# Batch 0's attention masks from TensorE to VectorE in a planned attention and feed-forward kernel, with new planner numbers

## The chip, the core and the metric

The kernel runs on one core of one Trainium2 chip. Its engines are TensorE (PE in the profile; PEld is its weight load), VectorE (DVE), ScalarE (ACT), GpSimd (POOL) and SyncE (SP), whose queue issues all DMA transfers. The metric is the device time of one execution in microseconds, as the median of several runs; lower is better.

## The reference

```
scores = scale * q @ k.T            # 8 batches, 8 heads, 576 positions, 64 wide
masks: heads 0-3 see the last 32 positions, heads 4-7 every 4th of the last 128
attn = softmax(where(mask, scores, -1e9)) @ v
x = attn as 4608 tokens x 512
h = x @ w_in                        # 512 -> 2048
g = (a0 + a1 h + a2 h^2 + a3 h^3) / (1 + |b0||h| + |b1| h^2 + 1e-6)
out = g @ w_out                     # 2048 -> 512
```

## The kernel before

**Attention** is cut into 8 batches of 6 units; unit n of the trace's names is 6 times the batch plus its place (`u`). A unit loads `qk` and `v`, and then runs these steps, each a planned operation: scores (`qk`, PE, into two PSUM banks named `pair`, `pair_A` or `pair_B`), mask, row maximum `mx` (DVE), subtraction into `p` (DVE), exponential (ACT), row sum `sm` and its reciprocal (DVE), normalisation of `p` (POOL), transposition to `pT`, and the product with `v` (PE). The result is split into a high part `xh` (ACT) and the rest `xl`, the two float32r operands of the feed-forward products; columns that belong to the last block of tokens are kept aside as `l` and stored to DRAM as `left`.

The mask is added in one of two ways, chosen by `on_pe`. With it, PE multiplies an identity `ident_b` with the bf16 mask `mask_t` into the bank before the scores are accumulated on top (two matmuls of 128x192 a unit). Without it, `mask()` adds the mask on DVE after the scores, in one instruction or two, by the list `MASK_AT`: two pieces in units 0, 4 and 5, one in units 1, 2 and 3.

The exponential has three kinds, in the table `KIND`. Kind 0: DVE subtracts the maximum into `p`, ACT takes one exponential of `p`, DVE sums. Kind 1: ACT takes six exponentials of 64 columns straight from the bank, each with a bias and an accumulated sum. Kind 2 (all of batch 1): PE subtracts the maximum in the bank with two matmuls.

**Feed-forward** is cut into 144 tiles: a block `c` of 512 tokens by a slice `ft` of 128 hidden columns. The order starts with block 0's first 8 slices, then block 1's 16, then block 0's other 8, then blocks 2 to 8. Tile i makes the hidden product `h` (12 matmuls of 128x512, called h0, h1 and so on below), then a chain: `a` = |h|, `r` (linear, ACT), `t` (linear, ACT), `a<-r,a` (DVE or POOL), two further products on DVE (`t<-t,h`, `h<-t,na_t,h`), logarithm and exponential of `r` (ACT), and three products on DVE, the last of which (`a<-a,h`, here "the last product of the tile") gives g and frees the bank of `h`. Then `gh` = g rounded (ACT, or POOL) and `gl` = g - gh (DVE or POOL for the first 36 tiles, POOL after), and the output products `out` (12 matmuls). The weights come as raw words (`wi_raw`, `wo_raw`) and are put together by ACT, POOL and DVE (`wi_f`), then split into `wi` high and low. Weight slots of the last slices first hold batch 0's `qk` and `v`.

**The order** of all instructions on all engines is made when the program is built, by `Plan.run`: a list scheduler that takes the operation of lowest rank among those that can start first, by durations written in each `op(...)`, hop times between engines and a model of the DMA pipe; where an operation may run on more than one engine it also picks the engine. Ranks come from `due()`, which goes back from due times (`DUE`, one pair a batch), lags in tiles (`LATE`) and margins (`SLACK`). `masked` is the load of the masks, `lc` that of the six coefficients, and `coefs` makes `na_t` (DVE) and `ab_t` (ACT) from them. `pin` keeps that order on each engine, so every engine and the SP queue works strictly in it.

Of the kernel before, what the change touches and what calls it, by code (L numbers as in the profile page):

```python
# [78 lines left out]
class Plan:  # L79
# [6 lines left out]
    DMA_START, DMA_NS, DMA_RATE = 3300.0, 1750.0, 375.0  # L86
# [97 lines left out]
def tile_attention_moe(  # L184
# [29 lines left out]
    def act(o, i, func, **kw):  # L214
        pin(nc.scalar.activation(o, i, func, **kw))  # L215
# [41 lines left out]
    class Unit:  # L257
        def __init__(self, b, u):
            self.b, self.u, self.n = b, u, b * NU + u
            self.start, self.on_pe, self.by_pe = b == 0, b < ON_PE, b < BY_PE  # L260
# [248 lines left out]
        def plan(self, by, tags):  # L509
# [10 lines left out]
            if prev:  # L520
                sc = op({"PE": 1320 + 300 * self.on_pe}, 0, lambda e: (prev.av(), self.scores()), *prev.placed, prev.lv, lq, *masks)
                clear = prev.finish(sc)
            else:
                sc = op({"PE": 1130 + 320 * self.on_pe}, 0, lambda e: self.scores(), lq, *masks)
# [54 lines left out]
            if start:  # L579
                av = op({"PE": 1500}, 0, lambda e: self.av(), *self.placed, lv)  # L580
# [5 lines left out]
        def finish(self, av):  # L586
# [331 lines left out]
    for key in keys:  # L918
        plan_weights(key)
# [127 lines left out]
```

## Time and profile before

| | |
|---|---|
| median of 3 runs | 916.32 us (913.51 to 917.98) |
| the profiled execution | 916.49 us, its span 914.7 us |
| mean granted TensorE clock | 0.994 |
| PE busy | 883.2 us, 97% of the span |
| DVE busy | 742.3 us, 81% |
| ACT busy | 675.4 us, 74% |
| POOL busy | 467.7 us, 51% |
| DMA | 103.46 MB, mean 113 GB/s |

The span runs from the first to the last instruction; times in the trace count from its start. A busy share is a mean over stages with different limits, so what a change is worth is read from the stage that it changes. PE works with pipelined matmuls whose ends are modelled: a busy PE is not always a PE at its peak, and the distance between two starts tells more than the busy time.

### The profile page before, as it was taken

The page shows a single profiled execution, that of the slowest core. Times are in us where ns is not written, and L with a number is a line of the kernel's source. Part 1 is how long each engine was busy: PE and PEld are TensorE (multiplying, and loading weights), DVE is VectorE, ACT ScalarE, POOL GpSimd, SP SyncE. Part 2 cuts the span into 40 slices and gives each one's busy share as a digit, 9 for nine tenths or more (in the row PEclk, how much of TensorE's full clock was granted, in tenths as well). Part 3 has the DMA queues.
Part 4 walks back from the last instruction along what each step waited for, and adds up shares of the span by engine and source line. Part 5 has one row for each costly group of instructions (what it writes and reads, how often), then busy time and mean ns, then how long its engine had stood idle before and what let it go on. Part 6 is the DMA issues. An engine that isn't in the chain of part 4 may idle for free.

```text
span 914.7 us, 21129 instructions
## 1 busy us (share of the span) xinstructions
PE 883.2 (97%) x8153; PEld 716.1 (78%) x8153; DVE 742.3 (81%) x1312; ACT 675.4 (74%) x1092; POOL 467.7 (51%) x408
## 2 busy tenths in 40 slices
PE   5877999999999999999999999999999999999998
PEld 3755787887877878888888888888888788888876
DVE  4789999999988988788978888887779677566656
ACT  2676888877666777877787778677777688778764
POOL 2454554656635554555455555546455545444442
PEclk9989999999999999999999999999999999999999
DMA  9667460235633343334334324423333220001001
GB/s 359 240 221 249 154 234 1 99 124 190 198 99 110 110 134 118 119 111 125 115 113 127 121 83 146 129 82 85 115 95 91 61 69 1 1 1 47 0 1 47
DMA packets 85477, 103.46 MB, mean 113 GB/s; under 512 B 37376, under 2 KB 62848, under 8 KB 85376
## 3 DMA queue, kind: packets, MB, share of 16 engines
q1 hardware_dynamic: 85376, 102.11, 34.5%
q8 instruction: 64, 1.05, 0.5%
q14 instruction: 37, 0.30, 0.1%
HBM read 75.21 MB, written 26.87 MB: 112 GB/s over the span
## 4 chain that ended last, share of the span: by engine, by line
PE 75%; DVE 11%; DMA 5%; ACT 5%; issue 3%; POOL 1%; SPq 1%; DVEq 0%; POOLq 0%; ACTq 0%
PE out L212 34%; PE h L212 34%; PE pair L212 5%; DVE h L221 3%; DVE a L221 2%; DMA wi_raw<-in_w_in_dram 2%; ACT r L215 2%; DVE t L218 1%; DVE a L218 1%; DVE gl L218 1%; DMA wo_raw<-in_w_out_dram 1%; SPq L209 1%; DMA qk<-in_qk_dram 1%; ACT a L215 1%; PE pair_B L212 1%
## 5 line engine op out<-in xcount | busy, mean ns | idle before, releaser
L212 PE MATMUL h<-xh,wi 128*128 128x512 f32 x1136 | 378.1, 394 | 6.8 <-DVE a L221 6.5
L212 PE MATMUL out<-gh,wo 128*128 128x512 f32 x1136 | 353.8, 393 | 0.7 <-DVE os L218 0.7
L224 POOL TENSOR_TENSOR a<-r,a 128x512 f32<-128x512 f32 x121 | 156.6, 1294 | 241.1 <-ACT r L215 233.4
L212 PEld LDWEIGHTS h<-xh,wi 128*128 128x128 f32 x1136 | 214.5, 189 | 58.3 <-DVE a L221 12.6
L212 PEld LDWEIGHTS out<-gh,wo 128*128 128x128 f32 x1136 | 211.2, 188 | 45.9 <-DVE os L218 1.1
L212 PE MATMUL out<-gl,wo 128*128 128x512 f32 x568 | 221.8, 391 | 1.6 <-DVE gl L218 1.0
L212 PE MATMUL h<-xl,wi 128*128 128x512 f32 x568 | 222.4, 391 | 0.0
L224 POOL TENSOR_TENSOR gl<-a,gh 128x512 fp32r<-128x512 f32 x129 | 175.1, 1357 | 64.7 <-ACT gh L215 64.0
L221 DVE SCALAR_TENSOR_TENSOR h<-h,na_t,r 128x512 f32<-128x512 f32 x142 | 106.9, 753 | 111.0 <-ACT r L215 109.2
L215 ACT ACTIVATE r<-a,ln_bias 128x512 f32<-128x512 f32 x141 | 101.9, 723 | 82.8 <-POOL a L224 80.3
L215 ACT ACTIVATE r<-a,ab_t 128x512 f32<-128x512 f32 x141 | 114.7, 814 | 16.3 <-DVE a L221 14.5
L212 PEld LDWEIGHTS out<-gl,wo 128*128 128x128 f32 x568 | 106.6, 188 | 25.6 <-POOL gl L224 1.5
L212 PEld LDWEIGHTS h<-xl,wi 128*128 128x128 f32 x568 | 107.3, 189 | 21.5
L215 ACT ACTIVATE a<-h 128x512 f32<-128x512 f32 x140 | 83.5, 596 | 53.7 <-PE h L212 35.0
L215 ACT ACTIVATE t<-h,na_t 128x512 f32<-128x512 f32 x142 | 109.6, 772 | 5.0 <-PE h L212 4.6
L221 DVE SCALAR_TENSOR_TENSOR h<-t,na_t,h 128x512 f32<-128x512 f32 x142 | 107.3, 756 | 4.9
L215 ACT ACTIVATE r<-r,exp_bias 128x512 f32<-128x512 f32 x144 | 104.3, 724 | 4.7
L218 DVE TENSOR_TENSOR t<-t,h 128x512 f32<-128x512 f32 x142 | 96.6, 681 | 7.2 <-ACT t L215 7.1
L221 DVE SCALAR_TENSOR_TENSOR a<-a,r 128x512 f32<-128x512 f32 x141 | 100.2, 711 | 0.0
L221 DVE SCALAR_TENSOR_TENSOR a<-a,h 128x512 f32<-128x512 f32 x140 | 96.2, 687 | 4.8
L215 ACT ACTIVATE gh<-a 128x512 fp32r<-128x512 f32 x130 | 81.5, 627 | 23.2 <-PE out L212 14.9
L224 POOL TENSOR_TENSOR p<-p,sm 128x384 f32<-128x384 f32 x48 | 47.7, 993 | 34.3 <-DVE sm L352 28.1
(115 smaller groups left out, 712.4 us busy)
## 6 DMA issues: line engine op xcount, KB each, us to landing
qk<-in_qk_dram SPq DMA_DIRECT2D x48, 448.0 KB, 5.0
v<-in_vp_dram SPq DMA_DIRECT2D x48, 384.0 KB, 3.7
out_dram<-os SPq DMA_DIRECT2D x36, 256.0 KB, 2.3
wi_raw<-in_w_in_dram SPq DMA_DIRECT2D x16, 512.0 KB, 6.1
wo_raw<-in_w_out_dram SPq DMA_DIRECT2D x16, 512.0 KB, 6.9
results<-y SPq DMA_DIRECT2D x42, 192.0 KB, 2.4
z<-results SPq DMA_DIRECT2D x168, 48.0 KB, 2.5
turned<-u SPq DMA_DIRECT2D x36, 192.0 KB, 2.0
```

The lines of the kernel that those rows point to most:

```text
L209: pin(nc.sync.dma_start(dst, src))
L212: pin(nc.tensor.matmul(o, lhs, rhs, start=start, stop=stop, skip_group_check=free))
L215: pin(nc.scalar.activation(o, i, func, **kw))
L218: pin(nc.vector.tensor_tensor(o, x, y, op))
L221: pin(nc.vector.scalar_tensor_tensor(o, x, s, y, op0, op1))
L224: pin(nc.gpsimd.tensor_tensor(o, x, y, op))
```

## The change

Four things change.

1. `on_pe` holds for batch 1 alone; DVE adds the masks of batch 0.
2. `KIND[4]` goes from 1 to 0: unit 4's maximum is subtracted on DVE, its exponential is one ACT instruction, its sum one DVE instruction.
3. The masks' load follows the first load of all (`qk` of unit 0), and the coefficients' load and the next two loads follow the masks.
4. Durations in the plan, the DMA model, `DUE`, `LATE` and `SLACK` get other numbers. These set the order only; no instruction's work depends on them.

```
-KIND = [0, 0, 0, 0, 1, 0] + [2] * 6
+KIND = [0, 0, 0, 0, 0, 0] + [2] * 6
...
-DUE = [(-41.16, 11.47), (-146.25, 19.43), (423.68, 72.57), (61.95, 5.87), ...
+DUE = [(-44.94, 13.4), (-40.09, 42.02), (421.32, 53.66), (48.0, 2.07), ...
...
-    DMA_START, DMA_NS, DMA_RATE = 3300.0, 1750.0, 375.0
+    DMA_START, DMA_NS, DMA_RATE = 1000.0, 1700.0, 380.0
...
-            self.start, self.on_pe, self.by_pe = b == 0, b < ON_PE, b < BY_PE
+            self.start, self.on_pe, self.by_pe = b == 0, b == 1, b < BY_PE
...
-            no = op({"POOL": 790}, 0, lambda e: self.norm(e), rc)
+            no = op({"POOL": 880}, 0, lambda e: self.norm(e), rc)
...
-            low = {"DVE": sum(120 + 2 * c[1] / 0.96 for c, _ in main)}
+            low = {"DVE": sum(200 + 2 * c[1] / 0.9 for c, _ in main)}
...
-    lc = op({"SP": 60}, -39.5, lambda e: load(coef_t, coef), dma=3000)
-    masked.follows.append(lc)
+    lc = op({"SP": 430}, -39.3, lambda e: load(coef_t, coef), dma=3000)
...
+    masked.follows.append(first_loads[0])
+    for o in (lc, *first_loads[1:3]):
+        o.follows.append(masked)
```

The number behind a name's letters is the unit, the slice or the tile; the one behind the underscore is a buffer's serial number.

The start of SP's queue, before:

```order
L209 DMA qk0_110<-in_qk_dram 128x896
L209 DMA v0_112<-in_vp_dram 128x768
L209 DMA qk1_114<-in_qk_dram 128x896
L209 DMA coef_t_95<-in_coef_dram 128x6
L209 DMA mask_t_89<-in_mask_dram 128x384
L209 DMA v1_121<-in_vp_dram 128x768
```

and after:

```order
L209 DMA qk0_110<-in_qk_dram 128x896
L209 DMA mask_t_89<-in_mask_dram 128x384
L209 DMA v0_113<-in_vp_dram 128x768
L209 DMA qk1_115<-in_qk_dram 128x896
L209 DMA v1_120<-in_vp_dram 128x768
L209 DMA coef_t_95<-in_coef_dram 128x6
```

The masks move ahead of unit 0's v, and the coefficients behind unit 1's v.

SP's queue some 20 rows on, where the raw weights of slice 4 (`wi_raw4`) are loaded and unit 2's left part is stored, before:

```order
L209 DMA qk7_147<-in_qk_dram 128x896
L209 DMA wi_raw4_508<-in_w_in_dram 128x512
L209 DMA v5_510<-in_vp_dram 128x768
L209 DMA v6_512<-in_vp_dram 128x768
L209 DMA v7_514<-in_vp_dram 128x768
L209 DMA left_80<-l2_518 128x2x64
```

and after:

```order
L209 DMA qk7_206<-in_qk_dram 128x896
L209 DMA v6_210<-in_vp_dram 128x768
L209 DMA v7_238<-in_vp_dram 128x768
L209 DMA left_80<-l2_478 128x2x64
L209 DMA wi_raw4_484<-in_w_in_dram 128x512
L209 DMA left_80<-l3_522 128x2x16
```

The weight load moves from ahead of three loads to behind a store that waits for unit 2's result.

DVE in tiles 13 and 14 (the products of the chain; `wo_f8` joins the words of a weight), before:

```order
L218 TENSOR_TENSOR a13_2026<-r13_2031,a13_2026 128x512
L218 TENSOR_TENSOR gl12_2045<-a12_1972,gh12_2037 128x512
L218 TENSOR_TENSOR t13_2043<-t13_2043,h13_1994 128x512
L221 SCALAR_TENSOR_TENSOR h13_1994<-t13_2043,na_t_96,h13_1994 128x512
L221 SCALAR_TENSOR_TENSOR h13_1994<-h13_1994,na_t_96,r13_2031 128x512
L221 SCALAR_TENSOR_TENSOR a13_2026<-a13_2026,r13_2031 128x512
L221 SCALAR_TENSOR_TENSOR a13_2026<-a13_2026,h13_1994 128x512
L221 SCALAR_TENSOR_TENSOR wo_f8_2017<-wo_f8_2017,wo_raw8_1856 128x512
L218 TENSOR_TENSOR a14_2074<-r14_2080,a14_2074 128x512
L218 TENSOR_TENSOR gl13_2096<-a13_2026,gh13_2088 128x512
```

and after:

```order
L218 TENSOR_TENSOR a13_2043<-r13_2055,a13_2043 128x512
L221 SCALAR_TENSOR_TENSOR h13_2009<-t13_2048,na_t_96,h13_2009 128x512
L413 STREAM_TRANSPOSE y12_2080<-pair_85 128x2x96 x2
L381 STREAM_TRANSPOSE u14_2086<-p14_1973 128x192 x2
L221 SCALAR_TENSOR_TENSOR h13_2009<-h13_2009,na_t_96,r13_2055 128x512
L221 SCALAR_TENSOR_TENSOR a13_2043<-a13_2043,r13_2055 128x512
L221 SCALAR_TENSOR_TENSOR a13_2043<-a13_2043,h13_2009 128x512
L221 SCALAR_TENSOR_TENSOR wo_f8_2007<-wo_f8_2007,wo_raw8_1803 128x512
L218 TENSOR_TENSOR a14_2096<-r14_2102,a14_2096 128x512
L227 CAST wo8_2123<-wo_f8_2007 128x512
```

The two subtractions `gl` have left DVE (they stand in POOL's row), two attention transpositions and a weight's rounding stand between the products instead.

More of the change, by code (lines that the diff above doesn't have):

```diff
@@ L520, in plan @@
             if prev:
[L521 removed]
+                sc = op({"PE": 1320 + 700 * self.on_pe}, 0, lambda e: (prev.av(), self.scores()), *prev.placed, prev.lv, lq, *masks)
                 clear = prev.finish(sc)
             else:
[L524 removed]
+                sc = op({"PE": 1500 + 450 * self.on_pe}, 0, lambda e: self.scores(), lq, *masks)
             if self.on_pe:
@@ L531, in plan @@
                 mx = op({"DVE": 470}, 0, lambda e: self.max(True), ma)
-                sb = op({"PE": 760}, 0, lambda e: self.sub_pe(), mx, identity)
+                sb = op({"PE": 950}, 0, lambda e: self.sub_pe(), mx, identity)
                 su = ex = op({"ACT": 480}, 0, lambda e: self.exp_s(), sb)
-                sm = op({"DVE": 470}, 0, lambda e: self.sum(), ex)
+                sm = op({"DVE": 510}, 0, lambda e: self.sum(), ex)
             elif kind:
@@ L540, in plan @@
                 su = op({"DVE": 500}, 0, lambda e: self.sub(), mx)
-                ex = op({"ACT": 425}, 0, lambda e: self.exp(), su)
-                sm = op({"DVE": 470}, 0, lambda e: self.sum(), ex)
+                ex = op({"ACT": 470}, 0, lambda e: self.exp(), su)
+                sm = op({"DVE": 510}, 0, lambda e: self.sum(), ex)
             rc = op({"DVE": 300}, 0, lambda e: self.recip(), sm)
-            no = op({"POOL": 790}, 0, lambda e: self.norm(e), rc)
+            no = op({"POOL": 880}, 0, lambda e: self.norm(e), rc)
             if self.by_pe:
-                tr = op({"PE": 690}, 0, lambda e: self.transposes(), no, identity)
+                tr = op({"PE": 900 if start else 600}, 0, lambda e: self.transposes(), no, identity)
                 pl = op(BOTH, 0, lambda e: self.place(e), tr)
@@ L579, in plan @@
             if start:
[L580 removed]
+                av = op({"PE": 2000}, 0, lambda e: self.av(), *self.placed, lv)
                 av.slack = 0.0
@@ L601, in finish @@
                 if LESS[u]:
-                    ms = op({"PE": sum(60 + 2 * c[1] / 1.6 for c, _ in main)}, 0, lambda e: self.less_hi(), eh, identity)
+                    ms = op({"PE": sum(150 + 2 * c[1] / 1.4 for c, _ in main)}, 0, lambda e: self.less_hi(), eh, identity)
                     ms.slack = 0.0
@@ L611, in finish @@
             else:
-                low["POOL"] = sum(100 + 2 * c[1] / 0.49 for c, _ in main)
+                low["POOL"] = sum(130 + 2 * c[1] / 0.45 for c, _ in main)
                 el = op(low, 0, lambda e: self.evac_lo(e), eh, lock=True)
@@ L695, in plan_weights @@
             sc = op({"ACT": 600}, 0, lambda e: w_scale(key), f)
-            lw = op({"ACT": 690, "POOL": 690}, 0, lambda e: w_low(key, e), f, consts)
-            jn = op({"DVE": 680}, 0, lambda e: w_join(key), sc, lw, lock=True)
+            lw = op({"ACT": 690, "POOL": 740}, 0, lambda e: w_low(key, e), f, consts)
+            jn = op({"DVE": 710}, 0, lambda e: w_join(key), sc, lw, lock=True)
             steps = [sc, lw, jn]
@@ L700, in plan_weights @@
             steps = [op({"DVE": 335}, 0, lambda e: w_copy(key), f)]
-        hi = op({"ACT": 550, "DVE": 460, "POOL": 620}, 0, lambda e: w_hi(key, e), steps[-1], lock=True)
-        lo = op({"DVE": 602, "POOL": 1280}, 0, lambda e: w_lo(key, e), hi, lock=True)
+        hi = op({"ACT": 550, "DVE": 460, "POOL": 680}, 0, lambda e: w_hi(key, e), steps[-1], lock=True)
+        lo = op({"DVE": 625, "POOL": 1350}, 0, lambda e: w_lo(key, e), hi, lock=True)
         plan.takes(steps[0], "stage", STAGE, [lo])
```

12 lines of the change are left out of this document (6 added, 6 removed).

## Prediction

> **What bounds the kernel now.** I read the page's busy shares first, then a table of stages, then who TensorE waits for, then the rows of one stage.
>
> ```profile
> PE 883.2 (97%) x8153; PEld 716.1 (78%) x8153; DVE 742.3 (81%) x1312; ACT 675.4 (74%) x1092; POOL 467.7 (51%) x408
> ```
>
> TensorE (PE) is busy for 883.2 of 914.7 us; 31.5 us are left to win. The stages say where (columns: stretch, length, then busy us of each engine).
>
> ```profile
> 7.10:40.00 32.90, 27.10 (x722) 21.61 (x721) 23.55 (x57) 16.42 (x49) 12.30 (x14) 1.00 0.78 292
> 40.00:60.00 20.00, 15.90 (x337) 12.18 (x336) 16.64 (x38) 14.81 (x28) 8.42 (x9) 0.83 0.88 303
> 60.00:90.00 30.00, 23.29 (x284) 17.97 (x284) 27.77 (x51) 19.87 (x35) 12.68 (x15) 1.00 0.68 233
> 90.00:110.00 20.00, 19.10 (x166) 14.81 (x164) 18.60 (x32) 17.12 (x29) 12.47 (x11) 0.91 0.40 128
> 110.00:134.00 24.00, 23.68 (x194) 19.45 (x195) 23.64 (x36) 20.73 (x34) 13.10 (x11) 1.00 0.65 228
> 134.00:163.00 29.00, 28.73 (x122) 22.21 (x122) 28.05 (x43) 24.70 (x40) 13.31 (x11) 1.00 0.07 30
> 210.00:260.00 50.00, 49.47 (x578) 39.99 (x577) 45.27 (x88) 37.48 (x63) 27.19 (x28) 1.00 0.59 184
> 260.00:350.00 90.00, 89.01 (x840) 71.76 (x838) 76.19 (x139) 65.50 (x104) 48.35 (x45) 1.00 0.36 110
> ```
>
> PE's gaps before 110 us are 7.1 + 5.8 + 4.1 + 6.7 + 0.9 = 24.6 of the 31.5. Three regimes. Until 40 us everybody waits in turn: VectorE (DVE) is idle for 9.35 us of 32.9. From 60 to 134 us DVE is the bound: 27.77 of 30.0, then 18.60 of 20, then 23.64 of 24, while PE loses 6.7 us in 60 to 90. From 134 to 163 us both look full; later DVE has slack. The waits of PE name DVE too; the last row, from the timeline, is the start of h5, tile 5's hidden product:
>
> ```profile
> PE pair_A L212 <- DMA mask_t<-in_mask_dram: 7.3, 1, 7.3
> PE h L212 <- DVE a L221: 6.5, 5, 3.4
> ...
> 89.19 0.50 PE L212 MATMUL h<-xh,wi 128*128 128x512 f32 x1 [3.35 <-DVE a L221]
> ```
>
> The stage of 134 to 163 us hides a loss that no idle column shows.
>
> ```profile
> 139.16 0.50 PE L212 MATMUL h<-xh,wi 128*128 128x512 f32 x1
> 144.96 0.50 PE L212 MATMUL h<-xh,wi 128*128 128x512 f32 x1
> 150.76 0.50 PE L212 MATMUL h<-xh,wi 128*128 128x512 f32 x1
> ...
> 842.36 2.72 PE h L212 x12
> 845.08 2.72 PE out L212 x12
> ...
> 139.62 0.69 DVE L218 TENSOR_TENSOR a<-r,a 128x512 f32<-128x512 f32 x1
> 140.22 1.10 DVE L218 TENSOR_TENSOR gl<-a,gh 128x512 fp32r<-128x512 f32 x1
> 145.42 0.69 DVE L218 TENSOR_TENSOR a<-r,a 128x512 f32<-128x512 f32 x1
> ```
>
> The hidden products h13, h14, h15 start 5.80 us apart, though a tile needs 2.72 + 2.72 = 5.44 us of PE, as late in the run. DVE's own loop repeats in 145.42 - 139.62 = 5.80 us: DVE sets the pace, and 1.10 us of it is the subtraction that makes gl. So the time is PE's work plus what DVE withholds up to about 160 us.
>
> The profiled execution took 916.49 us around its 914.7 us span; the median of the runs is 916.32, 0.17 less. I sum against 916.49.
>
> **The change, part by part.**
>
> (1) The start. The masks' transfer moves from fifth to second, and the first scores no longer wait for it.
>
> ```profile
> 7.31 0.48 PE L212 MATMUL pair_A<-mask_t,ident_b 128*128 128x192 bf16 x2 [7.31 <-DMA mask_t<-in_mask_dram]
> ...
> 0.72 0.38 SPq L209 DMA_DIRECT2D qk<-in_qk_dram  x1
> DMA to landing us min/median/max: 3.2/3.2/3.2
> ...
> 3.04 0.43 SPq L209 DMA_DIRECT2D v<-in_vp_dram  x1
> DMA to landing us min/median/max: 5.2/5.2/5.2
> ...
> 9.91 0.52 ACT L215 ACTIVATE p<-p 128x384 f32<-128x384 f32 x1 [2.58 <-DVE p L218]
> ```
>
> The first qk lands at 0.72 + 3.2 = 3.9 us, so scores may begin 3.4 us before 7.31. But the coefficients now stand behind unit 1's v, which landed at 3.04 + 5.2 = 8.2 us, and ScalarE (ACT) still makes ab_t from them ahead of the first exponential, as DVE makes na_t ahead of the first sum. That exponential thus starts near 8.4 instead of 9.91: 1.5 us. Bounds: 0 (the later qk transfers pace the units anyway) and 3.4. What is late next is unit 1's qk. I take 1.5, as a head start for DVE only.
>
> (2) Masks and unit 4. PE loses twelve matmuls; DVE gains the additions, the subtraction and the sum.
>
> ```profile
> 8.62 0.50 PE L212 MATMUL pair<-mask_t,ident_b 128*128 128x192 bf16 x2
> 9.05 0.97 PE L212 MATMUL pair<-qk 64*32 64x64 f32 x48
> ...
> L218 DVE TENSOR_TENSOR pair<-pair,mask_t 128x192 f32<-128x192 f32 x2 | 0.7, 362 | 0.0
> L218 DVE TENSOR_TENSOR pair<-pair,mask_t 128x384 f32<-128x384 f32 x1 | 0.5, 541 | 0.0
> L218 DVE TENSOR_TENSOR p<-pair_A,mx 128x384 f32<-128x384 f32 x2 | 1.1, 553 | 0.0
> L348 DVE TENSOR_REDUCE sm<-p 128x6 f32<-128x384 f32 x13 | 7.1, 544 | 1.8 <-ACT p L215 1.7
> ```
>
> PE: 6 units by 9.05 - 8.62 = 0.43 us make 2.6 us, worth nothing here, since PE waits in this stage. DVE: three units with two pieces, 6 by 0.362, and three with one, 3 by 0.541, are 3.8 us; unit 4 adds 0.553 + 0.544 = 1.1 (a small scalar step that it loses is left in); together 4.9 us. ACT drops six small exponentials and their accumulator reads for one step; ACT is no bound here, so zero, covered by its 16.5 idle us before 40. Where do DVE's 4.9 us go? They must fit into 9.35 us of idle time plus the head start. Bounds: -1.5 (all fit, head start kept) and +3.4 (none fits, 4.9 - 1.5). The idle time is waiting between steps of one unit, and the masks belong to other units, so they fill it; yet each mask also lengthens its own unit's chain. I take 0.
>
> (3) The order of the ramp. Rows of both orders times the mean of their form's row say how much DVE must do before a landmark: up to the last product of tile 3 (on which h5 waits; 3.4 us is the longest wait above) 8.3 us more than before; up to tile 9 1.9 us more, with the 4.9 us of (2) inside. So apart from the masks DVE does less by tile 9, and batch 1's last unit and unit 13 are served earlier. h5 will come late by some us and tiles 6 to 10 get that back. Bounds at tile 9: +1.9 less the 1.5 of (1), so +0.4, if DVE's idle time stays as it is; 0.4 - 4.9 = -4.5 if the masks' time disappears in it. I take 0 at tile 10: the nearest rows, 90 to 134 us, show an engine with no idle time to fill.
>
> (4) Tiles 10 to 24. gl leaves DVE altogether: 12 before, none after; GpSimd (POOL) makes all 141 plain ones.
>
> ```profile
> L218 DVE TENSOR_TENSOR gl<-a,gh x9: 686/1101/1119, 116.9 to 253.5; 128x512 fp32r<-128x512 f32 x9
> L221 DVE SCALAR_TENSOR_TENSOR a<-a,r x25: 649/682/1341, 113.8 to 258.1; 128x512 f32<-128x512 f32 x25
> ...
> L224 POOL TENSOR_TENSOR gl<-a,gh 128x512 fp32r<-128x512 f32 x129 | 175.1, 1357 | 64.7 <-ACT gh L215 64.0
> ```
>
> Without gl the loop of 5.80 is 4.70, below PE's 5.44: PE sets the pace. h13 to h17 gain 5 by 0.36 = 1.8 us; bounds 0 and, if tiles 21 to 24 gain alike, 3.2. I take 2.2. POOL has room (13.31 of 29 us busy), but a gl of 1.36 us instead of 1.10 makes the path from gh to out longer; the second tile of buffers covers that.
>
> (5) After 210 us. PE idles 0.53 of 50 and 0.99 of 90 us; DVE does less, attention units start at other places. Bounds +1.5 (new collisions of the same size) and -1.5 (all gone); I take -1.1. Tiles after 100 keep their order of work in all but single rows, and so does the end: 0.
>
> Sum: 0 + 0 + 0 - 2.2 - 1.1 = -3.3, so 913.2 by the profiled execution and 913.0 against the median.
>
> **The rivals.**
>
> *The ramp shrinks (908).* If the planner's new order also closes DVE's gaps, term (3) takes its -4.5 or so: 916.5 - 3.3 - 4.5 = 908.7, with some of (1) kept 908. For it: 9.35 idle us before 40 and 3.4 more in 40 to 60. Against: these are chains of small steps over three engines, and DVE's row before h5 has grown by 8.3 us.
>
> *The slower side: weights held behind a store (921).* On SP's queue wi4 now stands behind the store of unit 2's left part, which waits for ACT.
>
> ```profile
> 15.94 0.33 SPq L209 DMA_DIRECT2D wi_raw<-in_w_in_dram  x1
> DMA to landing us min/median/max: 9.9/9.9/9.9
> 27.40 3.42 SPq L209 DMA_DIRECT2D left<-l  x2
> ...
> 36.37 0.47 SPq L209 DMA_DIRECT2D wi_raw<-in_w_in_dram  x1
> DMA to landing us min/median/max: 4.4/4.4/4.4
> ```
>
> Before it was issued at 15.94 and landed at 25.8; the store went out at 27.40. A lone transfer took 4.4 us. Behind a store as late as that one it would land at 27.8 + 4.4 = 32.2; unit 2 stands some 2 us further ahead in the new order, so I say 30.2, 4.4 us late. ACT takes its conversion in order, ahead of unit 4's evacuation and unit 5's exponential; wi6 can repeat it. If that time is not refilled before h5, the ramp ends 4.4 us later and the masks lose their cover for as long: 916.5 + 4.4 + 3.4 - 3.3 = 921. It decides if it holds ACT for over 4 us. Against: units 6 to 8 had slack on PE, and other steps are ready on DVE.
>
> *gl on POOL frees nothing (917).* The rows above show a<-a,r at 649 at least and 1341 at most: such an operation, both inputs in SBUF, can stand for up to 0.66 us beside POOL's work. If each gl of POOL blocks DVE for its whole 1.36 us instead of the 1.10 saved, the loop is 6.06 instead of 5.80, tiles 13 to 17 lose 1.3 us, and (4) turns from -2.2 to +1.3: 916.5 + 1.3 - 1.1 = 916.7, say 917. The median of 682 beside a maximum of 1341 says that few are blocked. [...]
>
> *The change does not act.* That DVE adds masks is sure; that nothing moves in the end is the middle of the other cases.
>
> **How the numbers follow.** Forecast 0.45, its own range 910.5 to 916. Ramp shrinks 0.28. gl frees nothing 0.13. Weights held 0.12. The rest, 0.02, is anything else. About 0.5%, 4.6 us, is what a measurement tells from no change: faster is below 911.7, slower above 920.9. Faster: nearly all of the second case (0.27) and a quarter of the first (0.11), 0.38. Slower: most of the weights case and a little of others, 0.12. Same: 0.50. The range 905.5 to 920 leaves out the far ends of the ramp case and the worse half of the weights case.
>
> **What the profile after would show.** (1) First scores near 4 us, first exponential near 8.4 with ACT waiting for coef_t; wrong if it still starts near 9.9. (2) DVE idle before 40 us lower by about 4; wrong if h0 and S8 move by more than 5. (3) h5 at 92 to 96 (89.2 before) and tile 13 (139.16 before) starting within 2 us of that. (4) No gl on DVE, h13 to h17 spaced by 5.44, a<-a,r still about 0.68 in the median; wrong if the spacing stays at 5.8. (5) PE idle after 210 us below 1.5. The prediction fails most likely in (3): a hand count cannot place the waits of three engines to a few us.

## The result, and the profile after

The changed kernel takes 929.81 us (median of four runs, 925.72 to 931.77), the kernel before 917.15 (913.51 to 918.58, the three runs shown and one more): a ratio of 1.0151, 95% interval 1.0130 to 1.0171. It is slower by 1.5%. The forecast was 913.0 with a range up to 920.0; the time lies outside it, on the other side of the kernel before.

The profiled execution of the changed kernel took 928.49 us, its span 926.7: 12.0 us more than before. First the page's busy shares.

```profile
PE 886.0 (96%) x8141; PEld 717.4 (77%) x8141; DVE 744.3 (80%) x1313; ACT 674.6 (73%) x1079; POOL 476.0 (51%) x419
```

PE has twelve matmuls less and is busy 2.8 us longer. DVE does 2.0 us more. Neither sum says where 12 us went, so the same stages as before follow (stretch, length, busy us of PE, its weight load, DVE, ACT, POOL, then PE's granted clock, the DMA share and GB/s).

```profile
7.10:40.00 32.90, 24.07 (x610) 18.82 (x611) 25.17 (x63) 15.84 (x37) 11.24 (x12) 1.00 0.83 300
40.00:60.00 20.00, 15.53 (x383) 11.92 (x383) 17.32 (x34) 16.09 (x33) 9.01 (x9) 0.91 0.77 269
60.00:90.00 30.00, 25.27 (x373) 19.22 (x372) 26.56 (x49) 19.82 (x36) 11.94 (x12) 0.89 0.82 278
90.00:110.00 20.00, 14.81 (x54) 11.71 (x53) 15.92 (x26) 15.16 (x26) 8.40 (x7) 0.83 0.27 83
110.00:134.00 24.00, 21.86 (x96) 17.38 (x95) 21.48 (x36) 17.95 (x29) 14.97 (x12) 1.00 0.39 125
134.00:163.00 29.00, 28.98 (x219) 23.58 (x218) 27.80 (x46) 26.27 (x44) 19.84 (x16) 1.00 0.43 149
210.00:260.00 50.00, 47.79 (x568) 37.80 (x567) 45.76 (x90) 33.22 (x55) 26.86 (x25) 1.00 0.57 177
260.00:350.00 90.00, 87.97 (x924) 71.12 (x925) 78.74 (x151) 64.50 (x104) 51.74 (x50) 1.00 0.44 131
```

From 60 to 134 us, where DVE was the full engine before (27.77, 18.60 and 23.64 us), it now has pauses: 26.56, 15.92 and 21.48. PE loses with it: 14.81 of 20 us instead of 19.10 in 90 to 110. From 134 to 163 PE is full, as the prediction wanted. After 210 us PE idles 2.2 of 50 and 2.0 of 90 us instead of 0.5 and 1.0. PE's table of waits has the largest ones (us in all, how many, the longest):

```profile
PE h L212 <- DVE a L221: 8.2, 5, 5.2
PE pair_A L212 <- DMA qk<-in_qk_dram: 5.3, 2, 4.0
PE pair L212 <- ACT r L215: 3.3, 1, 3.3
```

PE's timeline shows where they stand, and what follows a long one (start, duration, the wait ahead of it in brackets).

```profile
3.95 0.97 PE L212 MATMUL pair_A<-qk 64*32 64x64 f32 x48 [3.95 <-DMA qk<-in_qk_dram]
...
80.75 0.91 PE L212 MATMUL pair<-v,pT 64*32 64x64 f32 x45 [3.35 <-ACT r L215]
...
97.82 0.80 PE L212 MATMUL h<-xh,wi 128*128 128x512 f32 x1 [5.19 <-DVE a L221]
98.42 0.63 PE L212 MATMUL h<-xl,wi 128*128 128x512 f32 x1
...
102.69 0.63 PE L212 MATMUL h<-xh,wi 128*128 128x512 f32 x1
103.11 0.75 PE L212 MATMUL out<-gh,wo 128*128 128x512 f32 x2
...
148.33 0.39 PE L212 MATMUL h<-xh,wi 128*128 128x512 f32 x1
...
153.77 0.49 PE L212 MATMUL h<-xh,wi 128*128 128x512 f32 x1
...
220.48 0.67 PE L212 MATMUL pair<-v,pT 64*32 64x64 f32 x44 [1.65 <-DVE y L413]
```

h5 starts at 97.82 instead of 89.19, after the longest wait of the run. Its twelve matmuls then take 103.11 - 97.82 = 5.29 us; at full pace, as at 842 us in before, they take 2.72 (before, h5 took 4.40 after a wait of 3.35). So this wait costs PE twice, once idle and once slow. In all PE idles 36.8 us between its matmuls instead of 27.9, 8.9 of the 12.0 us; 2.8 are PE working longer, though 2.6 us of mask products are gone, and 0.3 stand behind its last matmul. In the rows from 40 to 110 us the granted clock withholds 0.09 x 20 + 0.11 x 30 + 0.17 x 20 = 8.5 us, in those of before 0.17 x 20 + 0.09 x 20 = 5.2; by this estimate up to 3.3 us of the longer work are the lower clock.

By landmarks the 12.0 us come as +3.8 until h0, +4.8 from h0 to h5, +0.5 to h13, -2.5 to h24, +3.8 to h40, +1.6 to the end. So 8.6 stand at h5, and all of it is still there at h13 (+9.1).

What h5 waits for is seen on DVE's timeline.

```profile
93.79 0.68 DVE L221 SCALAR_TENSOR_TENSOR a<-a,r 128x512 f32<-128x512 f32 x1
96.16 1.02 DVE L218 TENSOR_TENSOR xl<-z,xh 128x64 fp32r<-128x64 f32 x2 [1.69 <-ACT xh L215]
97.09 0.68 DVE L221 SCALAR_TENSOR_TENSOR a<-a,h 128x512 f32<-128x512 f32 x1
```

The last row is the last product of tile 3, which frees h5's bank. Its inputs were ready at 94.47, but the rest `xl` of unit 11 stands ahead of it in the list, and that waits for ACT, which waits for the transfer z of unit 11 (landed at 95.63). DVE idles 1.69 us and works 1.02 more before it turns to the row that PE needs. The PE wait at 80.75 is alike: a subtraction for unit 12 stood behind `xl` of unit 8 on DVE, which idled 1.93 us at 74.54 for that unit's z. (The table names ACT for this wait; that it is the subtraction is seen when this row is moved, below.)

On SP's queue (issues only) three weight loads have come forward into this stretch.

```profile
61.44 0.42 SPq L209 DMA_DIRECT2D wi_raw<-in_w_in_dram  x1
...
62.94 0.58 SPq L209 DMA_DIRECT2D wi_raw<-in_w_in_dram  x1
...
75.10 0.33 SPq L209 DMA_DIRECT2D wi_raw<-in_w_in_dram  x1
75.53 0.84 SPq L209 DMA_DIRECT2D z<-results  x2
```

They are `wi_raw8` to `wi_raw10`, first needed at about 165 us; before, they were issued together at 78.68 behind `wo_raw7`. DVE joins the words of two of them, and splits one, ahead of tile 3's last product. The DMA share of 60 to 90 us has gone from 0.68 to 0.82.

### The profile page after: what moved, and what is told of

The parts are those of the page before. It is cut to its first block, busy times and chain, and to the rows that moved or that the text cites. A ratio compares the mean times of both kernels' runs of the same rounds, so it can differ in the third digit from the quotient of the medians.

```text
span 926.7 us, 21150 instructions
## 1 busy us (share of the span) xinstructions
PE 886.0 (96%) x8141; PEld 717.4 (77%) x8141; DVE 744.3 (80%) x1313; ACT 674.6 (73%) x1079; POOL 476.0 (51%) x419
## 4 chain that ended last, share of the span: by engine, by line
PE 72%; DVE 10%; DMA 8%; ACT 4%; SPq 3%; issue 2%; POOL 1%; DVEq 0%; ACTq 0%; POOLq 0%
PE h L212 34%; PE out L212 33%; PE pair L212 4%; DMA z<-results 3%; SPq L209 3%; DVE h L221 2%; DMA results<-y 2%; DVE a L221 2%; ACT r L215 1%; DVE t L218 1%; DMA wi_raw<-in_w_in_dram 1%; DMA turned<-u 1%; DVE a L218 1%; DMA coef_t<-in_coef_dram 1%; DVE wo L227 1%
## 5 line engine op out<-in xcount | busy, mean ns | idle before, releaser
L224 POOL TENSOR_TENSOR a<-r,a 128x512 f32<-128x512 f32 x117 | 151.5, 1295 | 247.6 <-ACT r L215 226.9
L224 POOL TENSOR_TENSOR gl<-a,gh 128x512 fp32r<-128x512 f32 x141 | 190.7, 1353 | 60.0 <-ACT gh L215 53.1
L221 DVE SCALAR_TENSOR_TENSOR a<-a,h 128x512 f32<-128x512 f32 x140 | 96.1, 686 | 4.7
L224 POOL TENSOR_TENSOR p<-p,sm 128x384 f32<-128x384 f32 x48 | 46.2, 966 | 29.7 <-DVE sm L352 28.6
```

The costliest lines, as they stand in the source:

```text
L221: pin(nc.vector.scalar_tensor_tensor(o, x, s, y, op0, op1))
L224: pin(nc.gpsimd.tensor_tensor(o, x, y, op))
```

## The experiments

Three questions: is it the mechanism (masks and unit 4 on DVE, masks second on the queue) or the order that came with the new numbers; if the order, is it single rows, the early weights, or the weights behind the store of `left` (the prediction's own rival); and what is gl on POOL worth by itself. For all kernels but three the plan decides as usual; either some steps then emit other instructions in their old places, or the list is edited by the few moves shown before the instructions are emitted. So those differ from their parent by nothing but these rows (helpers shift the line numbers). The ratios are against the kernel before on the same chip; landmarks are the start of the hidden product of that tile in the profiled execution.

| kernel | h0 | h5 | h10 | h13 | h24 | h40 | span | ratio (95%) |
|---|---|---|---|---|---|---|---|---|
| before | 41.9 | 89.2 | 122.6 | 139.2 | 203.5 | 301.1 | 914.7 | 1 |
| after | 45.7 | 97.8 | 130.6 | 148.3 | 210.1 | 311.5 | 926.7 | 1.0151 (1.0130-1.0171) |
| *in the order of before* | | | | | | | | |
| masks_old_order | 40.8 | 87.1 | 120.9 | 137.6 | 201.9 | 299.4 | 912.3 | 0.9997 (0.9986-1.0008) |
| masks_second_old_order | 39.9 | 88.0 | 121.4 | 137.9 | 201.9 | 299.9 | 914.0 | 0.9992 (0.9977-1.0006) |
| masks_old_order_second | 42.3 | 90.2 | 123.6 | 140.1 | 204.4 | 301.7 | 914.6 | 0.9998 (0.9987-1.0009) |
| gl_pool_old_order | 41.0 | 89.3 | 125.0 | 141.5 | 204.6 | 302.4 | 916.1 | 1.0006 (0.9992-1.0021) |
| early_weights_old_order | 41.4 | 94.3 | 127.3 | 143.8 | 209.1 | 306.7 | 919.9 | 1.0068 (1.0049-1.0088) |
| *planned anew* | | | | | | | | |
| old_code_new_numbers | 48.7 | 101.2 | 137.2 | 152.7 | 224.6 | 323.9 | 936.4 | 1.0237 (1.0219-1.0256) |
| new_code_old_numbers | 41.8 | 89.8 | 122.5 | 146.4 | 210.1 | 317.3 | 931.1 | 1.0178 (1.0163-1.0194) |
| one_duration_changed | 42.1 | 91.1 | 122.2 | 140.5 | 204.0 | 308.8 | 921.9 | 1.0084 (1.0062-1.0107) |
| *in the order of after* | | | | | | | | |
| pe_masks_new_order | 47.2 | 99.4 | 130.0 | 147.6 | 209.6 | 312.8 | 925.6 | 1.0144 (1.0124-1.0165) |
| sub12_ahead_of_z8 | 45.0 | 95.6 | 126.9 | 144.7 | 206.4 | 307.7 | 921.4 | 1.0128 (1.0094-1.0162) |
| last3_ahead_of_z11 | 45.9 | 95.9 | 127.7 | 145.5 | 207.2 | 307.9 | 921.6 | 1.0099 (1.0082-1.0115) |
| both_rows_moved | 45.9 | 96.1 | 128.8 | 146.6 | 208.3 | 308.4 | 923.1 | 1.0112 (1.0092-1.0132) |
| weights_ahead_of_left | 44.9 | 97.0 | 132.2 | 149.9 | 211.7 | 313.4 | 927.4 | 1.0140 (1.0127-1.0154) |
| late_rows_moved | 44.8 | 97.7 | 132.8 | 150.4 | 212.2 | 315.7 | 931.0 | 1.0142 (1.0125-1.0160) |
| early_weights_later | 47.1 | 98.5 | 135.9 | 153.7 | 215.4 | 320.7 | 934.4 | 1.0198 (1.0176-1.0219) |
| early_weights_later_rows | 46.6 | 94.0 | 131.0 | 148.8 | 210.5 | 315.0 | 929.3 | 1.0155 (1.0132-1.0177) |
| weights_behind_z11 | 46.2 | 92.7 | 130.4 | 152.7 | 215.5 | 316.3 | 930.5 | 1.0205 (1.0186-1.0224) |
| weights_and_unit5 | 48.2 | 92.9 | 131.4 | 153.6 | 216.7 | 320.1 | 935.7 | 1.0213 (1.0190-1.0236) |

A landmark comes from one execution, and it varies: late_rows_moved has the order of after on every queue until 210 us, and its h10 still comes 2.2 us later. So differences of a landmark under some 2 us say little; the ratios carry the verdicts.

### The mechanism or the order

**masks_old_order**: the kernel before, whose order stays row for row; within it DVE adds batch 0's masks and unit 4 is kind 0.

```
-            on_pe = self.on_pe
+            on_pe = self.b == 1
...
+            if self.start:
+                self.mask()
...
-                mx = op({"DVE": 660}, 0, lambda e: self.max_bank(), ma)
+                mx = op({"DVE": 660}, 0, lambda e: (self.max(), self.sub()), ma)
```

> The planned order of before, row for row, but VectorE adds batch 0's masks ahead of each maximum and unit 4 goes by subtraction, one exponential and a sum (the mechanism alone; the mask matmuls are left out of TensorE's rows). Theory A (the loss is in the re-made order: VectorE gets 9.6 us more work ahead of h5, of which the masks and unit 4 are 4.9): VectorE is idle 16.8 us before h0, so the masks fit mostly there: h0 within 2 us of 41.9, h5 within 2.5 of 89.2, time 915 to 920. Theory B (the masks themselves cost the loss, because each lengthens its unit's chain by 0.4 to 0.7 us and VectorE is the bound later): h0 4 us later, h5 6 to 9 us later, time 922 to 929.

**pe_masks_new_order**: the reverse, the order of after with the masks on PE and unit 4 as before (`bank` is true for unit 4).

```
-            on_pe = self.on_pe
+            on_pe = self.b < ON_PE
...
-                su = op({"DVE": 500}, 0, lambda e: self.sub(), mx)
-                ex = op({"ACT": 470}, 0, lambda e: self.exp(), su)
+                su = op({"DVE": 500}, 0, lambda e: None if bank else self.sub(), mx)
+                ex = op({"ACT": 470}, 0, lambda e: self.exp_bank() if bank else self.exp(), su)
```

> The planned order of after, row for row, but TensorE adds batch 0's masks again and unit 4 takes its six small exponentials (the mechanism undone, the order kept). Theory A: little comes back, h5 stays at 96 to 98, time 926 to 930. Theory B: most comes back, h5 at 89 to 92, time 917 to 922.

915.70 against 915.45 for the first, 928.43 for the second. The mechanism costs nothing in the old order, and undoing it gives nothing measurable back in the new one (1.0144 and 1.0151 overlap). The whole loss belongs to the order. How the masks are taken up shows in the first kernel's stage:

```profile
7.10:40.00 32.90, 24.14 (x712) 20.01 (x712) 28.78 (x71) 15.22 (x39) 12.49 (x15) 1.00 0.82 309
```

DVE works 28.78 us of 32.9 instead of 23.55: 5.2 us more, all in its idle time. The second kernel's stage and its h5:

```profile
7.10:40.00 32.90, 24.11 (x613) 18.71 (x614) 20.13 (x53) 16.23 (x46) 10.99 (x12) 1.00 0.80 292
```

```profile
99.43 0.79 PE L212 MATMUL h<-xh,wi 128*128 128x512 f32 x1 [5.85 <-DVE a L221]
```

Here DVE has 5 us less to do than after has in this stage, and h5 comes no earlier (99.43 against 97.82). How much DVE has to do before h5 does not alone set when h5 starts.

**old_code_new_numbers** (code of before, numbers of after) and **new_code_old_numbers** (code of after's parts 1 and 2, numbers and load order of before) are both planned anew, as is **one_duration_changed**, the kernel before with one planned duration, that of the row sum, 10 ns longer (it stands in two places, of which one is shown).

```
-                sm = op({"DVE": 470}, 0, lambda e: self.sum(), ex)
+                sm = op({"DVE": 480}, 0, lambda e: self.sum(), ex)
```

> The kernel before with the durations, transfer model, due times, lags and margins of after, so the planner makes the order anew with TensorE's masks. Theory A: the numbers carry the loss, 922 to 932, with h5 later than 93 and waits on z loads ahead of VectorE. Theory B: about 917, h5 at 88 to 91.

> VectorE adds batch 0's masks and unit 4 is changed, planned anew with all of before's numbers and before's order of the first loads. Theory A: near before, 914 to 920. Theory B: like after, 922 to 930.

> The kernel before with one planned duration changed from 470 to 480 ns (the row sum on VectorE), so that the planner makes the order anew: the same instructions, about 300 of 1218 rows of VectorE's order in another place. Theory T (the old numbers were fitted to the old program, and any new draw of the order loses): ratio 1.005 to 1.025. Rival N (the numbers of the change are bad in themselves): 0.998 to 1.004.

937.46, 931.75 and 924.09: 2.4, 1.8 and 0.8% slower. So neither set of numbers is good or bad by itself. The old numbers fit the old program only, and even there 10 ns in one duration, which by the plan moves some 300 of DVE's 1218 rows, cost 0.84%. Each of the four orders planned anew in this study, after's own included, was slower than before's. They do not lose in the same place: new_code_old_numbers is level with before until h10 (122.5), 7.2 us late at h13 and 16.1 at h40.

**masks_second_old_order** and **masks_old_order_second** put the masks' transfer second, in before's order and in that of masks_old_order.

```
+    def edit(self):
+        self.move("masked", ahead_of=("lv", 0))
```

> The order of before, row for row, but the masks' transfer is the second on the queue. Step (1) of the prediction: the first scores start near 4.3 instead of 7.31, the first exponential near 7.3; the later qk transfers land as before, so units 2 to 5 and h0 move by less than 0.5 us and the time by less than 1 us. Rival: the head start lasts and h0 is 1.5 to 3 us earlier, and so is the end.

> The order of before, VectorE adding batch 0's masks and unit 4 changed as in after, and the masks' transfer second on the queue. If both single moves keep what their profiles show (h0 1.1 and 2.0 us earlier), 912.5 to 915, ratio 0.997 to 0.9995; if the head start is lost to the later qk transfers, 0.999 to 1.001.

0.9992 and 0.9998: nothing that can be measured, alone or with the masks on DVE. The profiles of the two single moves had h0 1.1 and 2.0 us earlier, the one of both together has it 0.4 later. No version here beats the kernel before.

### gl on POOL

**gl_pool_old_order**: before's order, and DVE's twelve gl handed to POOL.

```
+        gl = {id(self.named["gl tile", i]) for i in range(36)}
+        self.order = [(o, "POOL" if id(o) in gl else eng) for o, eng in self.order]
```

> The order of before, row for row, but the 12 subtractions for gl that VectorE did (tiles 4 to 35) are done by GpSimd at the same place of the plan. Step (4) of the prediction: tiles 13 to 17 start 5.44 us apart instead of 5.80, the time falls by 1.8 to 3.2 us. [...]

1.0006. The faster pace is real, but less than 1.10 us are won: DVE's `a<-r,a` in tiles 13 to 15 stand 5.61 and 5.60 us apart instead of 5.80, and the product `a<-a,r` between them takes 1.18 us instead of 0.68:

```profile
141.56 0.68 DVE L232 TENSOR_TENSOR a<-r,a 128x512 f32<-128x512 f32 x1
...
144.75 1.18 DVE L235 SCALAR_TENSOR_TENSOR a<-a,r 128x512 f32<-128x512 f32 x1
...
147.17 0.69 DVE L232 TENSOR_TENSOR a<-r,a 128x512 f32<-128x512 f32 x1
...
152.77 0.69 DVE L232 TENSOR_TENSOR a<-r,a 128x512 f32<-128x512 f32 x1
```

h13 to h18 takes 27.7 instead of 28.9 us, but tile 13 starts 2.4 us late, h10 having been 2.5 late already, and at h24 1.1 us are still missing. What holds the tiles between h5 (on time) and h10 is not shown by itself; the stretched rows below, 3.1 us more than in before up to tile 9, are of that size. One price of POOL's gl is seen in DVE's rows on the weights (count, then least, median and most ns), here the rounding, first in before, then in after:

```profile
L227 DVE CAST wo<-wo_f x4: 426/427/428, 57.8 to 203.9; 128x512 fp32r<-128x512 f32 x4
```

```profile
L227 DVE CAST wo<-wo_f x9: 426/1403/1523, 59.0 to 216.1; 128x512 fp32r<-128x512 f32 x9
```

And the split, first in before, then in gl_pool_old_order, which gives POOL nothing but the twelve gl:

```profile
L218 DVE TENSOR_TENSOR wo<-wo_f,wo x5: 679/680/693, 56.5 to 83.1; 128x512 fp32r<-128x512 f32 x5
```

```profile
L232 DVE TENSOR_TENSOR wo<-wo_f,wo x5: 677/693/1655, 56.1 to 82.7; 128x512 fp32r<-128x512 f32 x5
```

The stretched rows stand beside a row of POOL: the cast from 216.10 to 217.62 beside gl from 215.77 to 217.34, the split of 1.66 us at 79.66, of which 1.11 overlap a gl.

Up to the last product of tile 9, DVE's rows on the weights (joining the words, rounding, splitting) take 2.2 us more in before than they would at the 0.43 us of an undisturbed rounding and the 0.69 of the others; in gl_pool_old_order they take 5.3 more, and in after 9.6. Of after's 41 such rows 16 are stretched (roundings over 0.54 us, others over 0.8), and all 16 overlap a row of POOL in time (gl, a step of attention or a weight's split); of before's 37 rows 5 are, and all 5 do.

In the products, `a<-a,r` keeps its 681 ns in the median of the whole run, yet in gl_pool_old_order it takes 1.18 to 1.22 us in tiles 13 to 16, where POOL is busy 18.89 us of the 29 from 134 to 163 us, instead of 13.31. In after:

```profile
L221 DVE SCALAR_TENSOR_TENSOR a<-a,r x141: 648/681/1698, 56.5 to 901.8; 128x512 f32<-128x512 f32 x141
```

So the prediction's row was right for most products, but the price fell also on these and on weight rows that it had not looked at.

### The waits ahead of h3 and h5

**sub12_ahead_of_z8** and **last3_ahead_of_z11** move one row each, **both_rows_moved** both.

```
+        self.move(("su", 12), ahead_of=("el", 8))       # unit 12's subtraction ahead of unit 8's xl
+        self.move(("g2 tile", 3), ahead_of=("el", 11))  # tile 3's last product ahead of unit 11's xl
```

> The order of after with one row moved: VectorE's subtraction of unit 12's maximum (which frees the bank that unit 11's product with v and unit 13's scores wait for) stands ahead of xl of unit 8, which waits until unit 8's z transfers land at 76.0. Theory Q (VectorE stands behind late transfers in its strict row, and TensorE behind VectorE): the wait of 3.35 us at 80.75 falls below 0.5, h3 starts 2.5 to 3.3 us earlier, h5 2 to 3 us earlier, time 1.5 to 3 us below after. Rival W (VectorE's sum of work sets h5): h3 is earlier, but h5 stays within 1 us and the time within 1 us of after (927 to 930).

> The order of after with one row moved: VectorE's last product of tile 3, on which h5 waits, stands ahead of the two subtractions that make xl of unit 11 and wait for z transfers that land at 95.63. Theory Q: h5 at about 95.3 instead of 97.8, half or more of it kept to tile 10, time 1 to 2.5 us below after. Rival W: h5 earlier, given back by h8; time within 1 us of after.

> The order of after with the two rows moved together: unit 12's subtraction ahead of xl of unit 8, and the last product of tile 3 ahead of xl of unit 11. Theory Q: the two waits add, since the first move alone brought h3 from 82.3 to 78.7 and left h5 waiting for z11; h5 at 92 to 94, ratio to before 1.005 to 1.009. Rival W: the ratio stays at that of the second move alone, 1.010.

928.52, 925.19 and 927.24. The first removes its wait (h3 at 78.7 instead of 82.3), yet h5 comes only 2.2 us earlier, after a still longer wait of 6.78 us, and the median barely moves (its profiled execution, 923.09, is its fastest by 5 us). The second is the largest gain found in the new order: 1.0099 instead of 1.0151, 0.5% for one row's place. Its DVE rows and h5:

```profile
95.20 0.69 DVE L234 SCALAR_TENSOR_TENSOR a<-a,h 128x512 f32<-128x512 f32 x1
96.09 1.00 DVE L231 TENSOR_TENSOR xl<-z,xh 128x64 fp32r<-128x64 f32 x2 [0.20 <-ACT xh L228]
```

```profile
95.95 0.50 PE L225 MATMUL h<-xh,wi 128*128 128x512 f32 x1 [1.94 <-DVE a L234]
...
98.84 0.61 PE L225 MATMUL out<-gh,wo 128*128 128x512 f32 x2
```

h5 is 1.9 us earlier, and its matmuls take 2.89 us instead of 5.29, after a wait of 1.94 us. Together that is 4.3 us at the end of h5. At h10 and h13 2.9 of them are left and the spans differ by 5.1, so that the medians differ by 4.6 is near it in part by chance. Both moves together gain nothing over the second alone. DVE's rows tell why:

```profile
84.83 0.65 DVE L427 STREAM_TRANSPOSE y<-pair 128x192 f32<-128x192 f32 x2 [1.55 <-DMA results<-y]
...
95.40 0.69 DVE L235 SCALAR_TENSOR_TENSOR a<-a,h 128x512 f32<-128x512 f32 x1
```

The chain runs ahead now and meets the next late transfer: unit 11's `y` waits for a buffer that unit 10's store frees at 84.73, on the queue behind two weight loads and unit 9's z. From there DVE works without a pause to 96.09, PE waits 5.06 us and starts slow again: h5's first two matmuls start 0.60 us apart, as in after, and not 0.34 as in last3_ahead_of_z11.

### The weights

**weights_ahead_of_left** tests the prediction's rival: the loads of slices 4 to 6 go ahead of unit 2's `left` store.

```
+        for n in (4, 5, 6): self.move(("wi", n), ahead_of=("lf", 2))
```

> The order of after with the loads of wi4, wi5 and wi6 ahead of the store of unit 2's left part on SP's queue. The prediction's rival (weights held behind a store): ScalarE's waits of 1.0, 0.7 and 1.6 us at 29.8, 32.9 and 39.2 vanish, h0 is 2 to 3.5 us earlier and the time 2 to 4.4 us lower. Theory Q with other places: h0 is set by unit 5's product with v, which stands on TensorE behind the subtraction of unit 7; h0 moves by less than 1.5 us and the time by less than 1.5 us.

h0 moves by 0.8 us, the median (929.50) not at all. ACT did wait for these weights in after, 0.99, 0.72 and 1.58 us at 29.81, 32.88 and 39.17; here two of these waits are gone and 0.50 us of the first is left. So it is not what the time hangs on: that rival falls.

**early_weights_old_order** puts the other suspect, the early loads and steps of slices 8 to 10, into before's order, the loads behind `wo_raw4` to `wo_raw6`.

```
+        for n, o in ((8, 4), (9, 5), (10, 6)):
+            self.move_behind([("wi", n)], ("wo", o))
+        self.move_behind([(s, "wi", 8) for s in ("scale", "low", "join", "hi", "lo")], ("g2 tile", 2))
+        self.move_behind([(s, "wi", 9) for s in ("scale", "low", "join")], ("t2 tile", 3))
+        self.move_behind([("low", "wi", 10)], ("g2 tile", 2))
+        eight = [id(self.named[s, "wi", 8]) for s in ("hi", "lo")]
+        self.order = [(o, "DVE" if id(o) in eight else eng) for o, eng in self.order]
```

> The order of before, but the loads of wi8, wi9 and wi10 behind those of wo4, wo5 and wo6, and the steps of wi8 and the first three of wi9 ahead of tile 3's last product (wi8's split on VectorE), about as in after. Theory E: h5 3 to 6 us later than 89.2, ratio 1.003 to 1.007. Rival W2: h5 within 1.5 us, ratio 0.999 to 1.002.

922.92, 0.68% slower: by itself this costs nearly half of what the change lost. h5 stands at

```profile
94.35 0.50 PE L236 MATMUL h<-xh,wi 128*128 128x512 f32 x1 [2.74 <-DVE a L245]
```

instead of 89.19, and 4.6 to 5.6 us of it remain at every later landmark and at the end.

**early_weights_later** undoes it in after: the loads go behind `wo_raw7`, their steps behind the last products of tiles 4 to 6. **early_weights_later_rows** has the two rows moved besides; **weights_behind_z11** has these two rows, the loads of slices 8 to 12 behind unit 11's z, and the steps spread over more tiles; **weights_and_unit5** has unit 5's rows 3 us earlier as well.

```
+        self.move_behind([("wi", n) for n in (8, 9, 10)], ("wo", 7))
+        for n in (8, 9, 10):
+            self.move_behind([(s, "wi", n) for s in ("scale", "low", "join", "hi", "lo")], ("g2 tile", n - 4))
...
+        self.move_behind([("wi", n) for n in (8, 9, 10, 11, 12)], ("got", 11))   # weights_behind_z11
```

> The order of after, but the loads of wi8, wi9 and wi10 (first needed by tiles 16, 17 and 18) stand behind that of wo7 on SP's queue, as in before, and their five steps on ScalarE, GpSimd and VectorE behind the last products of tiles 4, 5 and 6. Theory E (weights for tiles 16 to 18 taken ahead of tile 3's chain: three transfers of 512 KB ahead of the z and results transfers, 3.9 us of VectorE and a wait of 2.2 us on ScalarE ahead of h5): h5 at 90 to 93.5 instead of 97.8, ratio to before 1.006 to 1.010 instead of 1.015. Rival W2 (the ramp is set by the places of units 11 to 13): h5 at 96 to 98, ratio 1.013 to 1.017.

> The kernel of early_weights_later with the two moved rows of both_rows_moved as well. Theory E: the waits that both_rows_moved ran into were those of the early weights, so now both add: h5 at 87 to 91, ratio 1.001 to 1.007. Rival W2: no better than the better of the two, 1.010 to 1.012.

> The order of after with the two moved rows of both_rows_moved; the loads of wi8 to wi12 stand behind the z transfers of unit 11 on SP's queue; of wi8, wi9 and wi10 the scaling, the joining and the splitting stand behind the last products of tiles 5, 6 and 7 (one tile later for each further weight) instead of all in one place. Theory E with the queue: z10 lands at 85 to 87 instead of 90.9, no wait of over 1.5 us on VectorE between 75 and 97, h5 at 89 to 92, h8 at 109 to 113, ratio to before 1.001 to 1.007. Rival W2 (units 11 to 13 set the ramp by their places): h5 at 94 or later, ratio 1.010 or more.

> The kernel of weights_behind_z11 with unit 5's own steps, from its scores to its x, 3.0 us earlier in the plan (past unit 4's transposition, two weights' steps and unit 7's subtraction). If unit 5's rows hold h0, h0 is 2 to 3 us earlier than in weights_behind_z11 and the ratio 0.002 to 0.003 lower. If h0 is held by what the later qk transfers and code at the start allow, h0 within 1 us and the ratio within 0.001.

934.63, 930.59, 935.03 and 936.46: none better than after. In the first h5 does not come earlier at all (98.5); in the other three it comes 3.9 to 5.1 us earlier, and by h13 that is lost. In the first the weights land at 85.28, 87.70 and 89.87, and unit 10's z right behind them at 90.91; DVE shows it:

```profile
91.44 0.86 DVE L238 TENSOR_TENSOR xl<-z,xh 128x160 fp32r<-128x160 f32 x2 [4.00 <-ACT xh L235]
```

In weights_behind_z11 h5 comes at 92.73, 5.1 us earlier than in after, and then ACT stops at a row of slice 11's weight that stands early in its list:

```profile
98.75 0.76 ACT L247 ACTIVATE wi_raw<-wi_raw,low_bias 128x512 int32<-128x512 uint32 x1 [5.76 <-DMA wi_raw<-in_w_in_dram]
```

h6 is at 105.3 (106.0 in after) and h13 at 152.7 (148.3). A transfer moved on the queue leaves the rows that use it where they stood on the engines. Moving unit 5's rows did not bring h0 forward either (48.2).

### After 210 us

**late_rows_moved** takes away the waits at 220, 303 and 317 us by four moves.

```
+        self.move(("to", 13), ahead_of=("tr", 15))   # unit 13's y
+        self.move(("lv", 22), ahead_of=("lq", 24))   # and three loads behind
+        self.move(("lv", 23), ahead_of=("pl", 22))
+        self.move(("lq", 25), ahead_of=("pl", 22))
```

> The order of after with four rows moved after 200 us: VectorE's transposition of unit 13's result earlier (TensorE waits for it at 220.5), and three loads for later units behind the round trip through DRAM of units 21 and 22 on SP's queue (TensorE waits for their pT at 303 to 304 and at 317). Theory Q: the waits of 1.65, 1.56 and 0.42 us go, ratio to before 1.011 to 1.013 instead of 1.015. Rival W (VectorE or GpSimd take up what is gained): 1.014 to 1.016.

930.75. Those waits go or shrink; others of 0.5 to 1.3 us come at 231, 249, 260, 267 and 310. Again a wait removed is a wait moved.

## Why the prediction was wrong, point by point

**The step that failed is (3), the order of the ramp.** What failed is "h5 will come late by some us and tiles 6 to 10 get that back", with the bounds from +0.4 down to -4.5 built on it: 0 was taken, h10 came 8.0 late and h13 9.1. It rests on two things that the runs do not bear out.

First, each row was counted at its mean time in the old kernel, and the rows did not keep it. Up to the last product of tile 9 DVE was busy 6.5 us longer than before (110.2 against 103.7), where 1.9 were counted. The weight rows alone make up for more than this difference: they stand 9.6 us over their undisturbed time there, against 2.2 before, and the stretched ones stand beside rows of POOL. This goes with the order too, and not with the masks: 9.1 us in pe_masks_new_order, 2.4 in masks_old_order. Up to tile 3 the count seemed to hold (8.3 us counted, 9.7 measured until h5, 76.9 against 67.2 busy; h5 came 8.6 later), but 4.9 of the 9.7 are again stretched weight rows, so that it came near is in part luck.

Second, DVE's idle time was let only shrink; until h10 it grew by 1.8 us (25.3 against 23.6). The sum of an engine's work bounds the time only if it never waits; in a fixed list it waits whenever its next row does, and pe_masks_new_order and masks_old_order show that a landmark need not come earlier with less work nor later with more. One row's place (last3_ahead_of_z11) is worth 0.5%. How the 9.1 us split between stretched rows and waits is not shown.

The rival that was missing follows: a list planned anew is slower by itself, by 0.8 to 2.4% in every case tried. That the one before had been fitted to the waits of the chip is my reading of it; no run shows how its numbers came about. With (1) and (2) worth nothing in the old order, the loss at h13 is the order's.

**(1) The start.** Right in kind, mis-sized, and worth nothing as taken. The scores start at 3.95, and ACT and DVE wait for the coefficients as foretold; ACT's rows:

```profile
9.05 0.20 ACT L215 ACTIVATE ab_t<-coef_t 128x2 f32<-128x2 f32 x1 [7.05 <-DMA coef_t<-in_coef_dram]
9.16 0.51 ACT L215 ACTIVATE p<-p 128x384 f32<-128x384 f32 x1
```

The first exponential comes at 9.16, 0.75 before the old 9.91 and not 1.5. Unit 3's scores, 12.54 against 12.39, show that the head start is gone by then.

**(2) Masks and unit 4.** Right, and shown: 0 was taken, 0.9997 measured with the order held. In after DVE's idle time before 40 us went down by 1.6 us only (9.35 to 7.73) and not by the 4 foretold (in masks_old_order by 5.2), and h0 came 3.8 late; pe_masks_new_order has h0 later still (47.2), so that is not the masks.

**(4) gl off DVE.** The mechanism is there: h13 and h14 are 153.77 - 148.33 = 5.44 apart, and h13 to h18 took 27.6 us instead of 28.9. So 1.3 us of the 1.8 that these tiles were to give. To h24 it is 2.5 us in all, near the 2.2 taken, but partly by luck: PE has 96 attention matmuls less in that stretch than before (96 instead of 192, 1.1 us), which now stand after h24. By itself the step is worth nothing (gl_pool_old_order), since it is lost ahead of tile 13. The rival "gl on POOL frees nothing" is thus half right: in its result when the step stands alone, and in that DVE rows stretch beside POOL for a part of the products and the weight rows, not for every gl. That a gl holds DVE for its whole 1.36 us, no run shows: in before and after no DVE row takes more than 1.13 us over the least of its kind, and DVE's loop in gl_pool_old_order is 5.60 us, not the rival's 6.06. Beside a row of POOL some rows stretch and others do not. The 1341 ns of `a<-a,r` in before, at 120.16, stand beside a weight's split on POOL from 119.66 to 120.95; on DVE a split of gl_pool_old_order took 1655 ns beside gl, 693 at most in before, and the roundings 1403 in the median in after, 427 in before; but of after's 25 weight rows up to tile 9 that are not stretched, 7 overlap a row of POOL too. What decides it is not shown.

**(5) After 210 us.** Wrong by more than its bounds. From h24 to the end +5.4 us, against -1.1 (+1.5 at most): 2.6 of them are idle time of PE between its matmuls (5.3 against 2.7), 1.5 are the 96 attention matmuls from ahead of h24, and what makes up the rest, 1.3, is not shown. "New collisions of the same size" was the upper bound; there were more of them and longer ones, and that work of another stage could move in here was not thought of.

**Weights behind the store** was put as the slower side with 921. Its place and its waits on ACT were there, its price was not: 0.8 us at h0 and nothing in the median.

What stays open: what holds h0 back by 3.8 us (not the masks, of the weights behind the store at most 0.8, and not unit 5's rows, tried in the order of weights_behind_z11), and how the 12 us split among early weights, the place of single rows, rows stretched beside POOL and the late collisions. The single effects (0.7% and 0.5%) were measured in different orders and do not add.

## What to carry to other kernels

When a change re-plans a tuned list, price the new list first and the mechanism second: freeze the old order, apply the mechanism in it, and only then let the planner go. A count of work per engine is no bound from above on strict in-order queues (in after DVE idled 1.69 us ahead of `xl` while tile 3's last product, ready at 94.47, stood behind it); look for rows that wait on a transfer and stand ahead of the row that the bounding engine needs. A row's mean time from the old order need not hold in the new one (the roundings of `wo`: 427 ns in the median before, 1403 after): ask which row of POOL will stand beside it. And do not expect repairs to add up: each wait removed here uncovered the next one.

## What was not expected of the hardware

In these runs the length of PE's wait ahead of h5 went with the pace of what followed, but did not settle it. From the first start to the end of the last, h5's twelve matmuls took 2.88 to 3.06 us after waits of 0 to 1.94 us (old_code_new_numbers, new_code_old_numbers, last3_ahead_of_z11). After waits of 2.66 to 3.35 us they took 3.02 to 3.06 in three kernels and 4.50 to 4.61 in five; the same wait of 3.10 us was followed by 3.02 in weights_behind_z11 and by 4.60 in weights_and_unit5. After waits of 4.65 to 7.12 us it was 4.34 to 5.49 in all nine, with no order among them: 4.34 after 6.78 (sub12_ahead_of_z8), 5.49 after 5.19 (after). The granted clock of the stage from 90 to 110 us, 0.83 in after, is 1.00 in last3_ahead_of_z11. The shortest waits that were followed by slow matmuls are 2.66 and 2.74 us (one_duration_changed, early_weights_old_order). Why equal waits had unequal outcomes, no run shows. So near h5 a wait of over 4.6 us cost 1.3 to 2.4 us more than itself (against 3.06); by an estimate from these figures two waits under 2 us would be cheaper than one of 4.65, which no run here tests.
